# Eight weight images and the first routed tokens: a list scheduler's order for the work ahead of the first expert block

## The chip, the core and the metric

The kernel runs on one core of a Trainium2 chip. The metric is device time in microseconds (us) of one execution. Five engines work side by side, each through its own instruction stream: TensorE (PE; its weight loads are listed as PEld), VectorE (DVE), ScalarE (ACT), GpSimd (POOL) and SyncE (SP). Here SP mostly issues DMAs. An instruction waits at the head of its engine's stream until what it needs is there, and everything behind it in that stream waits too.

## What is computed

```python
# x: 8 x 3584 x 192, 8 heads of 24 columns, 7 taps per head
w = softmax(weight)                         # per head, over the 7 taps
out = np.einsum('hk,bskhg->bshg', w, x_unf) # causal convolution along the sequence
x = out.reshape(28672, 192)
logits = normalised(x) @ normalised(expert_emb).T / tau
expert_idx = np.argmax(logits, axis=1)      # one of 8 experts per token
gate_w = softmax(logits)[expert_idx]
for e in range(8):
    h = np.maximum(x[mask] @ w1[e], 0.0)    # 192 -> 1024
    out[mask] = gate_w[mask, None] * (h @ w2[e])  # 1024 -> 192
```

All inputs are fp32. The kernel multiplies in 16-bit floats: tokens, weights and hidden values are each scaled by a power of two and split into a high and a low half, and the products that matter are summed.

## The kernel before, in words

**Tokens.** The 28,672 tokens are 16 chunks of 1,792 (`CT`), each 16 tiles of 112. `mix` convolves a chunk: one matmul per head (L416) with a banded 128 x 112 matrix (`band`), copied back by ACT (L421); then the squares of each row (ACT L428, DVE L431) and an inverse root by a chain of small DVE instructions (L137 to L148, L440 to L444). `route` scales the chunk (DVE L460), casts the high half (ACT L462), subtracts for the low half (DVE L464, L467), turns the rows round (TensorE transposes L491 and ACT copies L495 for chunks 0 and 1, DMA transposes L617 for the others), multiplies with the expert vectors (L499), ranks (L518 to L573, ending in `di`, the target row of every token), and queues 16 scatters: GpSimd's indirect DMAs (L621) write each token's halves into `rows_d` in DRAM, sorted by expert.

**Experts.** `select` picks blocks of 128, 256, 512 or 1,024 rows of one expert, as soon as enough are there (`hand_out` after the chunk counts in `PICK`, the first after two chunks; `last_blocks` at the end). It leaves a table `sel` with the offset of the expert's weights and of the rows. `fetch` reads the row offset into a register of SP and issues a DMA transpose into `e_xT` (L741), which waits for the scatters it needs. `expert` runs one block: `flip` copies half of `e_xT` (L763), `copy_w1` and `copy_w2` copy the expert's images from `res` into the single `slot` (L723, L726) at an address in a DVE register that `value_load` (L720) has read from `sel`. Then h_ps (L796: five matmuls for 128 hidden columns), relu to a high half on ACT (L800) and the low half on DVE (L802), o_ps (L820: 24 matmuls for 128 rows), scaling by the gate (ACT L825) and a scatter into the output (POOL L827). The next block's W1 copy stands behind the last L802 of a block, its W2 copy behind the first steps of the next one.

**Weights.** For each expert SP loads W1 in two pieces and W2 (L290 to L292) into one of three staging buffers (parts of `slot`, `hid` and the end of `res`), so the load of expert e waits until expert e-3's images are finished. The sum of squares comes from matmuls (L321) and the diagonal (DVE L326; for the last four experts' W2 ACT squares), the scale from L156 to L162 and L334; the high half is written by ACT (L340), the low half by DVE (L344), both into `res`.

**What sets the order.** In `run` a hand-written interleaving (`HEAD`, `PRE`, `BEHIND`, `AHEAD`) issues weights, chunks 0 to 3 and a part of chunk 4 in turn; the framework's own scheduler then orders each engine's stream, except SP's, which keeps the order of the code. Once the first blocks are picked, `expert` yields after each step how much DVE and ACT time is left under the matmuls; `dispatch` spends it on later chunks at a pace `rate`, and `tick` issues one scatter per `pace` steps, at least `SPACE` us apart by the code's own clock.

## Time and profile before

| | us |
|---|---|
| three runs | 1281.48, 1278.87, 1280.43; median 1280.43 |
| the profiled execution | 1279.59 |
| its span, first to last instruction | 1277.9 |
| TensorE busy | 1162.7 (91%) |
| VectorE busy | 865.4 (68%) |
| ScalarE busy | 584.3 (46%) |
| GpSimd busy | 554.9 (43%) |

The span is what the profile's rows divide; 1.7 us of the execution lie around it. A matmul's listed time overlaps that of the next, so the distance of two starts is what a matmul costs in a row of them. "Idle before" is the time an engine stood still ahead of an instruction, with what ended it behind the arrow. `x_p_s` is a chunk's scale, `w_p_s` a weight's, `n` or `n2` a sum of squares.

### The profile page before, as it was taken

The numbers are of one execution on the slowest core, as the hardware profiler recorded it, in microseconds if no ns is written. First come the engines' busy times: TensorE is split into PE (matmuls) and PEld (weight loads), VectorE is DVE, ScalarE is ACT, GpSimd is POOL, SyncE is SP. The second block draws the span as 40 slices with busy tenths as digits, with TensorE's granted clock in tenths as the row PEclk, the third lists the DMA queues.
The fourth block names the chain that finished last, engine by engine and source line by source line (L and its number), as shares of the span: only waits on it lengthen the run. The fifth ranks groups of instructions, "written<-read, shape, count | busy, mean of one in ns | idle before, by whom it ended". The sixth has DMA issues, their size and how long they took to land. (4 is left out here: it accounts for less than half of the span.)

```text
span 1277.9 us, 29782 instructions
## 1 busy us (share of the span) xinstructions
PE 1162.7 (91%) x10852; PEld 927.9 (73%) x10852; DVE 865.4 (68%) x2274; ACT 584.3 (46%) x1343; POOL 554.9 (43%) x541
## 2 busy tenths in 40 slices
PE   4664689999999989999999989999999999999997
PEld 2542578788888878768886757667777777779997
DVE  2967758687877786857777566766644465466675
ACT  3967343544635444553545544543333333333332
POOL 0055054455555555455455544555555221223222
PEclk9666699999999999999999989999999999999999
DMA  9564536446454644645464256534323121111211
GB/s 261 149 195 115 109 91 118 105 107 150 98 124 103 138 100 111 157 101 124 93 137 114 87 125 139 110 90 92 80 65 82 43 52 38 45 38 42 49 43 23
DMA packets 274290, 129.15 MB, mean 101 GB/s; under 512 B 216110, under 2 KB 264621, under 8 KB 274144
## 3 DMA queue, kind: packets, MB, share of 16 engines
q1 hardware_dynamic: 250336, 80.39, 29.4%
q0 software_dynamic: 23808, 46.87, 12.9%
q8 instruction: 85, 1.39, 0.5%
q14 instruction: 61, 0.50, 0.2%
HBM read 38.35 MB, written 47.53 MB: 67 GB/s over the span
## 5 line engine op out<-in xcount | busy, mean ns | idle before, releaser
L820 PE MATMUL o_ps<-slot,hid 128*128 128x192 f16 x5544 | 500.9, 248 | 32.5 <-DVE hid L802 11.0
L820 PEld LDWEIGHTS <-hid 128*128 128x128 f16 x5544 | 460.6, 99 | 75.1 <-DVE hid L802 22.6
L796 PE MATMUL h_ps<-e_xT,slot 128*128 128x256 f16 (+2 forms) x3168 | 499.4, 292 | 10.9 <-DMA e_xT<-rows_d 7.3
L796 PEld LDWEIGHTS <-slot 128*128 128x128 f16 x3960 | 351.6, 99 | 168.8 <-issue 22.7
L827 POOL DMA_INDIRECT out_dram<-y,e_mt x231 | 267.0, 1156 | 432.8 <-ACT y L825 384.7
L802 DVE SCALAR_TENSOR_TENSOR hid<-h_ps,hid 128x512 f16<-128x512 f32 x462 | 310.1, 687 | 142.1 <-ACT hid L800 107.2
L800 ACT ACTIVATE hid<-h_ps 128x512 f16<-128x512 f32 x462 | 269.0, 597 | 220.0 <-PE h_ps L796 189.3
L621 POOL DMA_INDIRECT rows_d<-rows,di x256 | 269.6, 1053 | 226.0 <-PE h_ps L796 58.5
L796 PE MATMUL h_ps<-e_xf,slot 128*128 128x256 f16 (+2 forms) x792 | 219.0, 291 | 0.4 <-issue 0.4
L825 ACT ACTIVATE y<-o_ps,g 128x192 f32<-128x192 f32 x231 | 94.5, 420 | 266.7 <-PE o_ps L820 225.9
L726 DVE COPY slot<-res 128x3074 f16 x99 | 96.9, 979 | 120.3 <-PE o_ps L820 94.3
L416 PE MATMUL conv_ps<-xt,band 128*112 128x384 f32 x256 | 112.5, 548 | 18.7 <-ACT xt L421 7.4
L421 ACT COPY xt<-conv_ps 112x384 f32<-112x384 f32 x128 | 59.8, 479 | 84.4 <-PE conv_ps L416 49.1
L723 DVE COPY slot<-res 128x3072 f16 x99 | 94.2, 952 | 0.0
L462 ACT CAST rows<-xt 112x768 f16<-112x768 f32 x64 | 53.2, 832 | 85.7 <-DMA rows_d<-rows,di 60.7
L464 DVE TENSOR_TENSOR rows<-xt,rows 112x512 f16<-112x512 f32 x64 | 44.2, 691 | 45.8 <-ACT rows L462 41.0
L499 PEld LDWEIGHTS <-xT 128*112 128x112 f16 x768 | 55.8, 146 | 24.8 <-DMA xT<-rows 15.5
L416 PEld LDWEIGHTS conv_ps<-xt,band 128*112 128x112 f32 x256 | 43.3, 198 | 39.2 <-issue 16.8
L499 PE MATMUL lg_ps<-ma,xT 128*112 128x16 f16 x512 | 55.5, 202 | 15.8 <-DMA xT<-rows 14.1
L428 ACT ACTIVATE sq<-xt 112x192 f32<-112x192 f32 x192 | 68.3, 359 | 2.8 <-DVE sq L431 1.4
L460 DVE TENSOR_TENSOR xt<-xt,x_p_s 112x768 f32<-112x768 f32 x64 | 58.3, 951 | 0.2 <-issue 0.2
L763 DVE COPY e_xf<-e_xT 64x256 f16<-64x256 f16 (+2 forms) x198 | 46.5, 235 | 13.4 <-DMA e_xT<-rows_d 9.1
(163 smaller groups left out, 539.4 us busy)
## 6 DMA issues: line engine op xcount, KB each, us to landing
xt<-in_dram SPq DMA_DIRECT2D x39, 384.0 KB
xt<-in_dram SPq DMA_DIRECT2D x3, 1440.0 KB
rows_d<-rows,di POOLq DMA_INDIRECT x256
res<-in_dram SPq DMA_DIRECT2D x5, 768.0 KB
out_dram<-y,e_mt POOLq DMA_INDIRECT x231
xT<-rows SPq DMA_TRANSPOSE x224
xt<-in_dram SPq DMA_DIRECT2D x2, 1536.0 KB
hid<-in_dram SPq DMA_DIRECT2D x3, 768.0 KB
```

Source lines behind the costliest of these rows:

```text
L416: i = nc.tensor.matmul(out=ps, lhsT=self.band[:, h, :], rhs=xt[:, :, h * G:(h + 1) * G], start=True, stop=True).ins
L428: nc.scalar.activation(out=sq, in_=xc[:, t, :], func=AF.Square, accum_out=n2[:, t:t + 1])
L499: i = nc.tensor.matmul(out=lg[:, g * GX + a, :], lhsT=xT[:, a, k, :], rhs=self.mb if k == 1 else self.ma, start=(k == 0), stop=(k == 2)).ins
L621: i = self.nc.gpsimd.indirect_dma_start(out=self.rows_d[:, :], out_offset=bass.IndirectOffsetOnAxis(ap=idx, axis=0), in_=src, in_offset=No ...
L723: self.under(nc.vector.tensor_copy(out=self.slot[:, 0:W2], in_=v).ins)
L726: self.nc.vector.tensor_copy(out=self.slot[:, W2:], in_=self.res[:, bass.ds(self.we + W2, RES - W2)])
L796: self.mm = nc.tensor.matmul(out=ps[:, c, :], lhsT=w1(o, b + c), rhs=xk[k], start=(i == 0), stop=(i == 4)).ins
L800: self.step = nc.scalar.activation(out=hh[:, b:b + m, :], in_=ps, func=AF.Relu).ins
L802: self.low = nc.vector.scalar_tensor_tensor(out=hl[:, b:b + m, :], in0=ps, scalar=0.0, in1=hh[:, b:b + m, :], op0=ALU.max, op1=ALU.subtrac ...
L820: self.mm = nc.tensor.matmul(out=o, lhsT=h[:, c, q], rhs=w2[:, c, k:k + D], start=(c + i == 0), stop=(c == NFC - 1 and i == 2)).ins
L825: self.step = nc.scalar.activation(out=y, in_=o, func=AF.Copy, scale=g[:, a:a + 1]).ins
L827: i = nc.gpsimd.indirect_dma_start(out=self.out[:, :], out_offset=bass.IndirectOffsetOnAxis(ap=mt[:, a, 0:1], axis=0), in_=y, in_offset=No ...
```

## The change

The work ahead of the first block is now described as nodes: `chunk` and `weights` add each piece with its engine, a duration, what it needs and a priority, and `_Plan.run` repeatedly takes the node that could start first by these numbers and issues it. TensorE, VectorE and ScalarE keep that order. This head holds chunks 0 and 1 with their 32 scatters, of chunk 2 only the convolution, squares and root, all eight weights, the first pick and the first W1 copy; chunk 3 and a part of chunk 4 are no longer in it.

`res` becomes two tensors, `res1` for W1 and `res2` for W2. Expert e's weights are loaded into the place that expert e+2's images will take (the last two into `slot` and `hid`), so that no load waits for a staging buffer; the loads of x for chunks 2 and 3 wait for the splits of chunks 0 and 1. W1's last 64 rows come as 128 x 512. Chunks 0 and 1 in the head are cast with the scale on ACT, one tile per instruction, and DVE subtracts from the scaled product with two instructions per tile; nothing is scaled beforehand. Chunk 2 is turned round by TensorE as well. The first pick is followed by up to three 128-row blocks (`MORE`). The register load for a block is one instruction less and is tied behind the last L802 of the block before it, next to its copy.

```diff
-PRE = 14, 8
-BEHIND = 4
-HEAD = 9, 8, 9, 4, 2, 2, 2, 2
-AHEAD = 0.4
...
-MARGIN = 22
+MARGIN = 30
 KMAX = 32
+MORE = 3
+EAGER = 4
+DIRECT = 2
+FLIP = 1.5
+GRAMS = 4
...
+RANKS = 0.0, 0.28, 5.0
+ORDER = 0, ~0, ~1, 1, 2, ~2, 3, 4, 5, 6, ~3, 7
+PITCH = 1.4
+LATE = 1.0
+PICKED = 0.0
+ACTS = 6, 2, 14
 LAND_X, LAND_T = 9.0, 4.5
...
-SPACE, EVICT, SAVED = 1.65, 0.6, 8.0
+SPACE, EVICT, SAVED = 1.54, 0.6, 8.0
+SIGNAL, MOVED = 0.15, 1.8
+DONE = 2.6, 7.9
...
+    def run(self):
+        left = self.nodes
+        while left:
+            at = [(t + n.pri, k, t) for k, n in enumerate(left)
+                  for t in (self.start(n),) if t is not None]
+            _, k, t = min(at)
+            n = left.pop(k)
+            for r in n.takes:
+                self.rings[r][1].append(n)
+            if n.emit:
+                n.emit()
+            n.end = self.free[n.engine] = t + n.us
...
-        self.res = self.cp.tile([128, E * RES], F16, name="res")
+        self.res1 = self.cp.tile([128, E * IMG], F16, name="res1")
+        self.res2 = self.cp.tile([128, E * IMG], F16, name="res2")
...
+        nc.scalar.dma_start(out=sd, in_=seq)
+        self.band, self.cseq = cp.tile([128, H, TP], F32, name="band"), sd
+
+    def load_band(self):
+        run = self.cseq[:, 0:TP]
+        self.nc.sync.dma_start(out=self.band, in_=bass.AP(
             tensor=run.tensor, offset=run.offset,
             ap=[[1, 128], [2 * 128, H], [1, TP]]))
...
+    def stage(self, e):
+        n = 3 * F
+        if e < E - 2:
+            o = (e + 2) * IMG
+            t = self.res1[:, o:o + n], self.res2[:, o:o + n]
+        else:
+            t = (self.slot, self.hid)[e - E + 2]
+            t = t[:, 0:n], t[:, n:2 * n]
+        return [v.bitcast(F32) for v in t]
...
+                nc.sync.dma_start(out=v["st"][:, 0:F], in_=self.w1[e][0:128, :])
+                w = self.w1[e][128:192, :]
+                nc.sync.dma_start(out=v["st"][:, F:F + F // 2], in_=bass.AP(
+                    tensor=w.tensor, offset=w.offset,
+                    ap=[[F // 2, 2], [F, 64], [1, F // 2]]))
...
+        l1 = P.add("SP", 0.8, lambda: load(0), after, pri=pri)
+        m1 = self.move(3.0, l1, pri)
+        l2 = P.add("SP", 0.4, lambda: load(1), l1, pri=pri)
+        m2 = self.move(3.0, l2, pri)
+        a = P.add("PE", 1.3, lambda: gram(0), m1, takes=("h",), pri=pri)
+        a = P.add("DVE", 0.38, lambda: diag(0), a, back=((a, "h"),), pri=pri)
+        if e < GRAMS:
+            b = P.add("PE", 1.2, lambda: gram(1), m2, takes=("h",), pri=pri)
+            b = P.add("DVE", 0.38, lambda: diag(1), b, back=((b, "h"),), pri=pri)
+        else:
+            b = P.add("ACT", 1.66, square, m2, pri=pri)
+        n = P.add("PE", 0.4, total, a, b, takes=("h",), pri=pri)
+        n = P.add("DVE", 0.6, scale, n, takes=("wp",), back=((n, "h"),), pri=pri)
+        s, lows = n, []
+        for k, (t, u) in enumerate(((1.1, 1.25), (0.7, 0.75), (0.7, 0.75),
+                                    (1.5, 1.8))):
+            late = pri + (LATE if k == 3 else 0.0)
+            h = P.add("ACT", t, lambda k=k: high(k), n,
+                      *(clear[3:] if k == 3 else clear[:3]), pri=late)
+            lows.append(P.add("DVE", u, lambda k=k: low(k), h, pri=late,
+                              back=((s, "wp"),)))
+        return lows, l2
...
+        def cast(g):
+            for t in range(g, g + GX):
+                self.mark = nc.scalar.activation(
+                    out=rows[:, t, 0:D], in_=xc()[:, t, :], func=AF.Copy,
+                    scale=v["s"][:, t:t + 1]).ins
+
+        def rest(g):
+            for t in range(g, g + GX):
+                for a, b, o in ((0, 128, 256), (128, 192, 192)):
+                    nc.vector.scalar_tensor_tensor(
+                        out=rows[:, t, o:o + b - a], in0=xc()[:, t, a:b],
+                        scalar=v["s"][:, t:t + 1], in1=rows[:, t, a:b],
+                        op0=ALU.mult, op1=ALU.subtract)
...
+        subs, lgs, first = [], [], None
+        for g in range(0, NT, GX):
+            n = P.add("ACT", 1.3, lambda g=g: cast(g), s, pri=pri)
+            subs.append(P.add("DVE", 1.35, lambda g=g: rest(g), n, pri=pri))
...
+        for t in range(NT):
+            n = P.add("POOL", PITCH, lambda t=t: send(t), n, pri=pri)
+            sent.append(n)
+        return subs, done, sent
...
-    def route(self, c, xbar):
+    def route(self, c):
...
-            if xbar and 0 < g <= 2 * GX:
+            if c > DIRECT and 0 < g <= 2 * GX:
...
-        self.we = nc.vector.value_load(sel[0:1, j, 0:1], min_val=0,
-                                       max_val=(E - 1) * RES)
-        v = self.res[:, bass.ds(self.we, W2)]
+        (i,), (self.we,) = nc.values_load_multi_w_load_instructions(
+            sel[0:1, j, 0:1], engines=[nc.vector.engine], min_val=0,
+            max_val=(E - 1) * IMG, skip_runtime_bounds_check_because="select clamps it")
+        self.under(i.ins)
+        v = self.res1[:, bass.ds(self.we, W2)]
         self.under(nc.vector.tensor_copy(out=self.slot[:, 0:W2], in_=v).ins)
 
...
-            out=self.slot[:, W2:], in_=self.res[:, bass.ds(self.we + W2, RES - W2)])
+            out=self.slot[:, W2:], in_=self.res2[:, bass.ds(self.we, IMG)])
...
             0, -((E * (n - 1) - self.left) // n))
+        k = min(k, most)
...
+    def head(self, first):
+        P = self.plan = _Plan(
+            dict(h=5, r=2, l=1, x=2, root=1, wp=2),
+            dict(PE=8.6, DVE=8.8, ACT=7.6, SP=2.0, DMA=2.3, POOL=3.3))
+        moved, subs, ranked, sent = [], [], [], []
+        self.line, low = (), []
+        at = P.add("SP", 0.0, None)
+        self.banded = P.add("DMA", 0.0, None, lag=MOVED)
+        for k, v in enumerate(ORDER):
+            if k == 1:
+                at = P.add("SP", 0.4, self.load_band, at)
+                self.banded.after = self.move(2.5, at, 0.0),
+            if v >= 0:
+                l, at = self.weights(v, at, low[v - 2] if v > 1 else (), TURNS[v])
+                low.append(l)
+                continue
+            c = ~v
+            at = P.add("SP", 0.9, lambda c=c: self.load_x(c), at,
+                       *(subs[c - 2] if c > 1 else ()), pri=1.0)
+            moved = [self.move(5.4, at, 1.0)]
+            if c < first:
+                u, r, t = self.chunk(c, moved, RANKS[c], ACTS[c], ranked)
+                subs.append(u)
+                ranked.append(r)
+                sent += t
+            elif c == first:
+                self.chunk(c, moved, RANKS[c], ACTS[c], ranked)
+
+        def pick():
+            self.left = first * CT
+            self.hand_out(first)
+
+        def more():
+            self.subs += sum(self.pick(128, most=MORE), [])
+
+        n = p = P.add("DVE", 3.8, pick, ranked[-1], pri=PICKED)
+        for _ in range(3):
+            n = P.add("SP", 2.0, lambda: self.fetch(), n, *sent, at)
+        n = P.add("DVE", 1.3, lambda: self.copy_w1(0), p,
+                  *[v for l in low for v in l[:3]])
+        P.add("DVE", 4.2, more, n, *[l[3] for l in low], pri=2.0)
+        P.run()
+        self.asked = {c: -LAND_X for c in range(4)}
+        self.sp_at = 0.0
+
...
-        self.now = self.counts[c]
+        self.now, self.need = self.counts[c], NT * c
...
-        self.rate = min(self.rate, 3.0)
+        self.rate = 3.0 if self.end <= EAGER else min(self.rate, 3.0)
...
+        with self.tc.manual_schedule(engines={
+                e.tensor.engine, e.vector.engine, e.scalar.engine}):
+            self.head(first)
+        a, spent = self.dispatch(first), list(DONE)
```

`_Node` holds a piece's engine, duration, emitter, predecessors, buffer rings and priority; the emitters that the cut leaves out issue the instructions named above. Over the whole program TensorE's matmul transposes go from 96 to 144 and DMA transposes of x from 224 to 208; W1 and W2 copies go from 99 to 101 each (128-row blocks 21 to 25, 256-row blocks 51 to 49, 512-row pieces 27 as before); the output tiles stay 231 and the scatters of tokens 256.

SyncE at the start, before (`xt` is a chunk of x, `cseq_d` and `band` make the banded matrix, the others are weights):

```order
L369 DMA xt<-in_dram 112x192
L378 DMA xt<-in_dram 128x15x192
L227 DMA cseq_d<-cseq 8x256
L290 DMA slot<-in_dram 128x1024
L291 DMA slot<-in_dram 64x1024
L292 DMA res<-in_dram 128x8x192
L231 DMA band<-cseq_d 128x8x112
L290 DMA hid<-in_dram 128x1024
L291 DMA hid<-in_dram 64x1024
L292 DMA hid<-in_dram 128x8x192
L378 DMA xt<-in_dram 128x16x192
```

and after (`res_94` is `res1`, `res_95` is `res2`):

```order
L381 DMA res_94<-in_dram 128x1024
L383 DMA res_94<-in_dram 128x1x512
L377 DMA res_95<-in_dram 128x8x192
L310 DMA band<-cseq_d 128x8x112
L470 DMA xt<-in_dram 112x192
L479 DMA xt<-in_dram 128x15x192
L479 DMA xt<-in_dram 128x16x192
L381 DMA res_94<-in_dram 128x1024
L383 DMA res_94<-in_dram 128x1x512
L377 DMA res_95<-in_dram 128x8x192
L381 DMA res_94<-in_dram 128x1024
```

The band now follows the first weight, and x of chunks 0 and 1 come behind it, ahead of the second weight; the write of `cseq_d` has gone to ScalarE's queue.

VectorE at the first block, before:

```order
L344 SCALAR_TENSOR_TENSOR res<-hid,w_p_s,res 128x8x192
L723 ISA
L723 COPY slot<-res 128x3072
L148 SCALAR_TENSOR_TENSOR x_r_y<-x_r_t,x_r_y 112x16
L518 TENSOR_REDUCE l<-lg_ps 112x128
L726 ISA
L726 COPY slot<-res 128x3074
L763 COPY e_xf<-e_xT 64x256 x2
```

and after:

```order
L434 SCALAR_TENSOR_TENSOR res_94<-hid,w_p_s,res_94 64x512 x2
L434 SCALAR_TENSOR_TENSOR res_94<-slot,w_p_s,res_94 64x512 x2
L1094 COPY e_xf<-e_xT 64x256 x2
L1049 TENSOR_LOAD sel_3584_1058
L1054 ISA
L1054 COPY slot<-res_94 128x3072
L434 SCALAR_TENSOR_TENSOR res_95<-hid,w_p_s,res_95 128x8x192
L434 SCALAR_TENSOR_TENSOR res_95<-slot,w_p_s,res_95 128x8x192
L985 TENSOR_TENSOR sl_av<-cb_1025,start 1x8
L1133 SCALAR_TENSOR_TENSOR hid<-h_ps,hid 128x512
```

The flip of the fetched rows (`e_xf`) now stands ahead of the first W1 copy, and two low halves of W2 stand behind that copy, ahead of the first L802 (L1133 after the change).

VectorE at a 128-row block near the end, before:

```order
L811 TENSOR_SCALAR g<-e_mt,slot 128x1
L802 SCALAR_TENSOR_TENSOR hid<-h_ps,hid 128x512 x2
L723 ISA
L723 COPY slot<-res 128x3072
L763 COPY e_xf<-e_xT 64x128 x2
L726 ISA
```

and after:

```order
L1142 TENSOR_SCALAR g<-e_mt,slot 128x1
L1133 SCALAR_TENSOR_TENSOR hid<-h_ps,hid 128x512 x2
L1049 TENSOR_LOAD sel_1920_14585
L1054 ISA
L1054 COPY slot<-res_94 128x3072
L1094 COPY e_xf<-e_xT 64x128 x2
```

A TENSOR_LOAD now stands between the block's last low half and the W1 copy; before, the registers had been read in bunches behind each `select`.

## Rows read from the trace of the kernel before

**Rows 1.** Windows of all engines: length, busy us (x instructions), granted clock, DMA share, GB/s.

```profile
0.00:147.50 147.50, 81.64 (x510) 55.84 (x511) 99.66 (x332) 94.04 (x207) 39.61 (x57) 0.69 0.61 173
147.50:250.00 102.50, 94.15 (x899) 81.10 (x899) 69.42 (x208) 43.06 (x106) 42.83 (x40) 0.96 0.47 99
250.00:1000.00 750.00, 721.77 (x6527) 566.43 (x6527) 529.36 (x1440) 349.40 (x844) 395.82 (x379) 0.99 0.48 109
1000.00:1278.00 278.00, 265.10 (x2919) 224.50 (x2916) 166.99 (x294) 97.77 (x187) 76.68 (x65) 1.00 0.18 41
```

**Rows 2.** Timeline (start us, us, engine, line, operation, idle before), TensorE, first expert matmuls.

```profile
147.56 3.15 PE L796 MATMUL h_ps<-e_xT,slot 128*128 128x256 f16 x14 [2.64 <-DMA e_xT<-rows_d]
```

**Rows 3.** Waits in 0 to 147.5 us, SyncE queue: total us, times, longest.

```profile
SPq L290 <- DVE res L344: 42.7, 4, 18.2
```

**Rows 4.** Timeline, TensorE, first convolution.

```profile
16.69 7.00 PE L416 MATMUL conv_ps<-xt,band 128*112 128x384 f32 x16 [2.64 <-issue]
```

**Rows 5.** Groups by form, VectorE, 0 to 147.5 us: count, busy us, mean ns, idle before.

```profile
L460 DVE TENSOR_TENSOR xt<-xt,x_p_s 112x768 f32<-112x768 f32 x16 | 14.5, 949 | 0.2 <-issue 0.2
L464 DVE TENSOR_TENSOR rows<-xt,rows 112x512 f16<-112x512 f32 x16 | 11.0, 689 | 0.0
L467 DVE TENSOR_TENSOR rows<-xt,rows 112x256 f16<-112x256 f32 x16 | 6.8, 423 | 0.0
L344 DVE SCALAR_TENSOR_TENSOR res<-hid,w_p_s,res 128x1024 f16<-128x1024 f32 x3 | 3.9, 1285 | 0.0
L344 DVE SCALAR_TENSOR_TENSOR res<-res,w_p_s 128x1536 f16<-128x1536 f32 x5 | 9.0, 1802 | 0.1
L326 DVE SCALAR_TENSOR_TENSOR w_dg<-tr_ps,idf 128x128 f32<-128x128 f32 x12 | 3.5, 289 | 24.9 <-ACT sq L428 10.3 <-remote 8.9 <-PE tr_ps L321 5.2
```

**Rows 6.** Timeline, GpSimd, two scatters of chunk 1, the later one its last.

```profile
106.17 0.94 POOL L621 DMA_INDIRECT rows_d<-rows,di  x1 [0.31 <-issue]
...
117.35 1.42 POOL L621 DMA_INDIRECT rows_d<-rows,di  x1 [0.30 <-issue]
```

**Rows 7.** Timeline, SyncE queue, first fetch of a block.

```profile
144.41 1.24 SPq L741 DMA_TRANSPOSE e_xT<-rows_d  x1
```

**Rows 8.** Timeline, VectorE, the longest idle stretch after 30 us.

```profile
91.76 0.29 DVE L326 SCALAR_TENSOR_TENSOR w_dg<-tr_ps,idf 128x128 f32<-128x128 f32 x1 [7.90 <-remote]
```

**Rows 9.** Timeline, TensorE: one head of a convolution, twelve logit matmuls, eight transposes.

```profile
59.07 0.91 PE L491 MATMUL tr_ps<-idh,rows 112*128 112x112 f16 x8
...
194.67 0.17 PE L499 MATMUL lg_ps<-ma,xT 128*112 128x16 f16 x1
...
195.22 0.20 PE L499 MATMUL lg_ps<-ma,xT 128*112 128x16 f16 x1
...
730.58 0.82 PE L416 MATMUL conv_ps<-xt,band 128*112 128x384 f32 x2
731.24 1.98 PE L820 MATMUL o_ps<-slot,hid 128*128 128x192 f16 x22
```

**Rows 10.** Timeline, VectorE, around register loads.

```profile
816.34 0.18 DVE L145 TENSOR_TENSOR x_r_t<-x_r_y 112x16 f32<-112x16 f32 x1 [0.52 <-DVE x_r_y L148]
...
822.53 0.69 DVE L802 SCALAR_TENSOR_TENSOR hid<-h_ps,hid 128x512 f16<-128x512 f32 x1 [0.36 <-issue]
823.41 0.69 DVE L802 SCALAR_TENSOR_TENSOR hid<-h_ps,hid 128x512 f16<-128x512 f32 x1 [0.19 <-issue]
```

**Rows 11.** Timeline, VectorE, W1 copies behind a 256-row and a 128-row block.

```profile
1172.19 0.95 DVE L723 COPY slot<-res 128x3072 f16 x1
...
1191.40 0.95 DVE L723 COPY slot<-res 128x3072 f16 x1
```

**Rows 12.** Timeline, TensorE, first matmuls of the blocks behind those copies.

```profile
1174.71 0.39 PE L796 MATMUL h_ps<-e_xT,slot 128*128 128x128 f16 x4
...
1192.40 0.29 PE L796 MATMUL h_ps<-e_xT,slot 128*128 128x128 f16 x2
```

**Rows 13.** Waits in 147.5 to 1278 us, TensorE for fetched rows.

```profile
PE h_ps L796 <- DMA e_xT<-rows_d: 7.3, 3, 4.2
```

479 lines of the change are left out of this document (327 added, 152 removed).

## The prediction

> **What bounds the kernel now.** I read the windows first, then TensorE's timeline at their seams, then the waits, the groups by form and single timelines. The windows [rows 1] part the span in two. Up to 147.5 us no engine is full: TensorE 82 us busy, VectorE 100, ScalarE 94, at a granted clock of 0.69 on average. Then the first expert block starts [rows 2], and TensorE sets the pace: 1081.0 of 1130.5 us busy. Its 49.5 us of idle time are 8.4 to 250 us, 28.2 over the 750 us in which later chunks are worked in, and 12.9 after 1000 us. So a microsecond taken off the head is a microsecond off the span, unless it only moves TensorE's work behind 147.56, where it comes back one to one.
>
> Why the head is long: SP's queue holds weight loads back until a staging buffer is free, 42.7 us in four waits [rows 3], and VectorE, with the most work, is idle for 147.5 - 99.7 = 48 us.
>
> **The head, worked out.** Two chains end at the first block, and I count both.
>
> VectorE. Of its 99.7 us of work [rows 1] half of four chunks' scaling and subtracting leaves the head: (14.5 + 11.0 + 6.8)/2 = 16.2 [rows 5], and with chunk 3's squares and root some 4 more. The two chunks that stay change form: before 8.1 us a chunk; now 32 instructions of 112 x 128 and 112 x 64. The nearest row is the 128 x 128 form at 0.29 [rows 5]; two at that price are 9.3 us a chunk, at 0.29 and half of it 7.0. I take 8, no change. The weights' low halves cost what they cost: 1.29 for W1's first part, as much for its two halves of 64 rows, 1.80 for W2, 4.4 an expert. That leaves 79.5 us. W0's low halves (4.4) now run while x is on its way; the rest, 75 us, needs chunk 0's convolution. That began at 16.69 and took 7.00 [rows 4]; the band is now issued behind one weight and ahead of x, where before two weights and x surrounded it, so I leave the start at 16.7 (15 to 18). 23.7 + 75 = 98.7. The start-up's small instructions, which I have left in the 75, stand for the idle time that remains. Before, there were 48 us of it; the loads that caused most of it wait no more.
>
> Scatters. The last nine of chunk 1 took (117.35 - 106.17)/8 = 1.40 each [rows 6], 32 take 45 us. Ahead of chunk 0's `di` stand in VectorE's new order its own split (8) and squares, root and rank (about 9), of chunk 1 the squares and a quarter of its split, and one W1: some 25 us, with a few of waiting `di` at 51. 51 + 45 = 96. The fetch took 147.56 - 144.41 = 3.15 [rows 7, 2]. Then, by the new order, the flip of the fetched rows, the register load and the first W1 copy (0.95, [rows 11]) follow on VectorE in turn, 1.7 together, where before the copy was long done. 96 + 3.2 + 1.7 = 101.
>
> Both chains say about 100; I take 101 for the first h_ps, 94 to 112. Gain: 147.56 - 101 = **46.5 us**.
>
> **What comes back behind it.**
> - TensorE work that had been in the head: chunk 2's 48 logit matmuls: twelve start within 0.55 us (194.67 to 195.22, [rows 9]), 0.6 with the last, so 2.4; its rows are turned by 48 TensorE transposes instead of DMAs, 0.70/8 = 0.088 each in the head [rows 9], where the mean clock was 0.69 of full [rows 1], so 2.1 (if it was the lower of the levels, 1.2 against 2.4 GHz) to 4.2, I take 3.0; chunk 3's eight heads at 0.66 (730.58 to 731.24, [rows 9]), 5.3; three heads of chunk 4, 2.0. Sum **+12.7**.
> - The two W2 low halves behind the first W1 copy delay the first block's low halves by 2 x 1.80. Five PSUM banks cover part: **+2** (0 to 4).
> - Working in chunks costs TensorE idle time: (8.4 + 28.2)/13 = 2.8 for each of the 13 chunks worked in by then. About 1.75 chunks' work more: +4.9. Against it, `MARGIN` 22 to 30 lets scatters end earlier, and of 7.3 us of waits for fetched rows the longest is 4.2 [rows 13]: -4. The bunches of register loads behind each `select` are gone from VectorE; of some 100 loads at a quarter microsecond I give back a tenth, -3 (0 to -8). Sum **-2**.
> - Each load now stands between a block's last low half and the next W1 copy. A load shows as 0.52 us between two dependent instructions, and as 0.19 behind a long one [rows 10]. A 256-row block has room: its copy ends at 1172.19 + 0.95 = 1173.14 and the next block starts at 1174.71 [rows 11, 12]. A 128-row block has none: copy from 1191.40, h_ps at 1192.40, as soon as it ends. So it is paid at the 25 blocks of 128 rows: 25 x 0.19 = 4.8 to 25 x 0.52 = 13. Behind the long low half the shorter price is the nearer one; at 0.25, **+6**.
> - Two blocks more (four more of 128, two fewer of 256), each exposing a W1 copy of 0.95: **+2**.
>
> At nothing I cost the split of `res` in two (the copies keep their size), the SP issues (SP is not waited for once the loads flow) and ScalarE's finer casts: 94 us busy in the head before, less two chunks' casts and copies, it has room below VectorE's end.
>
> Sum: -46.5 + 12.7 + 2 - 2 + 6 + 2 = **-25.8**. The profiled execution took 1279.6 (span 1277.9 and 1.7 around it), 0.8 less than the median of the runs shown: 1279.6 - 25.8 = 1253.8, so **1254**.
>
> The Trainium skill has a figure that speaks against this change: "DMA: Bandwidth & Descriptors", section "Latency and other measured facts", gives a register load a floor of about 600 ns. By it the 25 loads would cost 15 and the sum would be 1263. The rows here are below it, 0.52 at most, so the trace does not agree and decides.
>
> **Rivals.**
> - *The queue at block ends is dearer.* Each load stops VectorE in full, 25 x 0.52 = 13 instead of 6; the new work in the first blocks (chunk 2's split, ranks and scatters, chunk 3's convolution) crowds VectorE and ScalarE, and TensorE's idle time to 200 us doubles from about 8. -25.8 + 7 + 8 = -10.8: 1269. For it: VectorE is 68% busy from 147.5 to 250 even before. Against: it has more room where blocks of 256 follow one another.
> - *The head does better.* First h_ps at 94, loads hidden but for 0.1 each, idle time per chunk falls by half a microsecond: -25.8 - 7 - 3.5 - 6 = -42: 1237. For it: if VectorE never waits, its chain ends at 92 to 94. Against: the scatters' 1.40 is a floor from the same trace and ends at 96 unless `di` comes sooner than 51.
> - *Slower: stalls under dense loads.* One idle stretch of 7.90 us hit VectorE with a releaser that the profile cannot name [rows 8]. Now all loads run densely from the start. If such stalls come with loads in flight, four of them (31.6) exceed the 25.8: 1285. Four is the point from which it decides; one in 147 us, none other as long in the head, speaks against four in a head of 100.
> - *It doesn't arrive.* The first hand-out is 7 blocks of 256 and 3 of 128 rows, 17 output tiles; 231 tiles in 1130.5 us are 4.9 each, so it lasts 83 us at most. Chunk 2 must have its 16 scatters out by then; before, it was ranked soon after the first block. If chunk 2's rows came 25 us late, TensorE would stand that long: 1279. Against: its scatters take 16 x 1.54 = 25 by `SPACE`, so there are over 50 us for the rest.
>
> **How the numbers follow.** About 0.2% (2.6 us) is what a measurement of this kernel can tell from no change. Forecast 0.55 (own range 1244 to 1264), dearer block ends 0.20, better head 0.14, stalls 0.06, gain not arriving 0.05. Faster: the first three and a little of the last, 0.90; same 0.04; slower 0.06. The unknown ends (first h_ps 94 to 112, loads 4.8 to 13, idle time) span from 1237 to 1272; leaving a tenth on each side gives 1238 to 1270.
>
> **What would show it.** First h_ps near 101 and chunk 0's convolution still from about 16.7; no wait of SP's loads for low halves but for x of chunks 2 and 3; the last scatter of chunk 1 near 96, and flip, load and W1 copy in turn behind the fetch; no second stall like the 7.90 one; near the end 0.2 to 0.3 between a 128-row block's last low half and its W1 copy, and the next h_ps later by as much; TensorE's idle time from the first block on near 50 to 60. If the first h_ps comes after 115, or that idle time passes 75, the sum is wrong, and the step is named by which of the two it is.

## The result, and the profile after

The change was forecast at 1254 us (1238 to 1270) and came out slower than before: 1290.8 us (median of 14 runs, 1279.5 to 1295.1) against 1281.0 for the kernel before, measured with it (14 runs), a ratio of 1.0056 (95% interval 1.0036 to 1.0075). The profiled execution took 1287.05, its span 1285.3.

The windows of the kernel after the change, cut at its first expert matmul, with the columns of [rows 1]:

```profile
0.00:132.00 132.00, 58.89 (x410) 43.08 (x410) 88.46 (x340) 76.94 (x147) 42.86 (x55) 0.71 0.57 172
132.00:250.00 118.00, 101.96 (x956) 83.60 (x957) 95.73 (x313) 66.20 (x191) 43.44 (x42) 0.89 0.41 97
250.00:1000.00 750.00, 724.96 (x6567) 568.28 (x6565) 527.82 (x1425) 349.20 (x831) 392.70 (x379) 0.99 0.49 109
1000.00:1285.30 285.30, 272.86 (x3021) 231.69 (x3018) 172.76 (x305) 99.95 (x191) 78.52 (x66) 1.00 0.19 42
```

The first window should end near 101 and ends at 132: the head became 15.4 us shorter [rows 2], not 46.5. TensorE is 22.7 us less busy in it than before [rows 1], and what was moved is paid behind it: from the first block to the end it is 1285.3 - 132.2 = 1153.1 us, against 1130.3 before. That is 22.8 more, where 20.7 were forecast (+12.7 +2 -2 +6 +2). Nearly the whole surprise, 31 us of 33, is in the head. VectorE has 88.5 us of work there and stands still for 43.5, nearly as long as before (48), though no weight load waits for a staging buffer any more [rows 3].

What keeps it waiting is seen in the windows of 10 us (the same columns):

```profile
70.00:80.00 10.00, 6.79 (x62) 6.16 (x61) 8.66 (x25) 8.60 (x15) 6.98 (x6) 0.50 0.68 202
80.00:90.00 10.00, 3.14 (x16) 1.70 (x16) 2.74 (x10) 3.66 (x4) 3.55 (x4) 0.50 0.85 259
...
100.00:110.00 10.00, 0.61 (x4) 0.34 (x4) 2.11 (x3) 4.78 (x6) 1.69 (x2) 0.50 0.09 28
```

From 80 to 90 and again from 100 to 110 us the five engines do little: VectorE is busy 2.7 and 2.1 us of 10. The timeline of the kernel after the change around these two holes, lines of all engines in order of time (start, us, engine, line, operation, idle before; SPq is SyncE's DMA queue):

```profile
80.85 1.03 PE L392 MATMUL tr_ps<-slot 128*128 128x128 bf16 x8 [2.30 <-DMA slot<-in_dram]
...
83.49 6.35 SPq L381 DMA_DIRECT2D hid<-in_dram  x1
...
87.57 0.61 PE L392 MATMUL tr_ps<-slot 128*128 128x128 bf16 x4 [5.68 <-DMA slot<-in_dram]
87.98 0.21 PE L681 MATMUL pc_ps<-rc,lth 112*128 112x8 f16 x1
...
88.28 0.17 DVE L687 TENSOR_TENSOR off<-pc_ps,cb 112x8 f32<-112x8 f32 x1 [7.12 <-PE pc_ps L681]
...
89.89 0.53 SPq L383 DMA_DIRECT2D hid<-in_dram  x1
...
102.66 0.61 PE L392 MATMUL tr_ps<-hid 128*128 128x128 bf16 x4 [5.37 <-DMA hid<-in_dram]
...
105.17 1.48 ACT L401 ACTIVATE hid<-hid 128x1536 f16<-128x1536 f32 x1 [13.15 <-DMA hid<-in_dram]
...
106.65 4.09 ACT L429 ACTIVATE res<-res,w_p_s 128x1024 f16<-128x1024 f32 x4
...
107.82 2.84 DVE L434 SCALAR_TENSOR_TENSOR res<-res,w_p_s 128x1024 f16<-128x1024 f32 x3 [8.19 <-ACT res L429]
...
108.68 1.24 POOL L950 DMA_INDIRECT rows_d<-rows,di  x1 [8.23 <-ACT res L429]
...
124.43 1.22 POOL L950 DMA_INDIRECT rows_d<-rows,di  x1 [0.30 <-issue]
...
127.31 1.34 SPq L1072 DMA_TRANSPOSE e_xT<-rows_d  x1
...
130.42 0.46 DVE L1094 COPY e_xf<-e_xT 64x256 f16<-64x256 f16 x2 [5.59 <-DMA e_xT<-rows_d]
131.15 0.96 DVE L1054 COPY slot<-res 128x3072 f16 x1 [0.28 <-DVE e_xf L1094]
132.17 1.03 PE L1127 MATMUL h_ps<-e_xT,slot 128*128 128x256 f16 x4 [4.71 <-DVE slot L1054]
```

In both holes TensorE waits for the second piece of a W1, the one that L383 loads: eight of the twelve matmuls of its sum of squares have run, the last four stand 5.68 and 5.37 us longer. Everything queued behind them stands too. At 87.57 these are chunk 1's rank sums (`pc_ps`), and with them VectorE (7.12 us). At 102.66 the queue is ScalarE's: the square of the last weight's W2, loaded behind that W1, has held ScalarE for 13.15 us, so the high halves behind it come late, for these VectorE waits 8.19 us and GpSimd, whose scatters are tied to ScalarE's order, 8.23. The last scatter starts at 124.43, and from the fetch on it goes as forecast: fetch, flip, copy, matmul, 4.86 us from 127.31 to 132.17 (3.15 + 1.7 forecast, [rows 7, 11]).

Why the second piece comes late is seen in windows of 1 us near the start, when the rest of the first weight has landed and only this piece is under way. After the change:

```profile
7.00:8.00 1.00, 0.58 (x6) 0.32 (x3) 0.00 (x0) 0.00 (x0) 0.00 (x0) 1.00 0.98 257
...
9.00:10.00 1.00, 0.00 (x0) 0.00 (x0) 0.00 (x0) 0.00 (x0) 0.00 (x0) 1.00 0.13 50
```

The last two columns: a DMA share of 0.13, what two fully busy ones of the 16 DMA engines make (2/16 = 0.125), at 50 GB/s. At that rate a piece of 256 KB takes 5.2 us (an estimate: 262,144 bytes at 50 GB/s), eight times in the head. The diff had it in plain sight: the source of L383 is `[[F // 2, 2], [F, 64], [1, F // 2]]`, two halves of a row outermost. The Trainium skill states the rule ("DMA: Bandwidth & Descriptors", section "Why a DMA increments its semaphore by 16 and not by 1"): the number of engines is the largest, up to 16, that divides the size of the slowest dimension (longer than one) of both sides. That makes two here, whatever the 128 partitions of the destination would allow. The trace agrees with its 0.13. The forecast had not put this load to that rule.

### The profile page after: what moved, and what is told of

Read it like the earlier page. It is cut to its first block, busy times and chain, and to the rows that moved or that the text cites. A ratio compares the mean times of both kernels' runs of the same rounds, so it can differ in the third digit from the quotient of the medians.

```text
span 1285.3 us, 29875 instructions
## 1 busy us (share of the span) xinstructions
PE 1158.7 (90%) x10948; PEld 926.7 (72%) x10948; DVE 884.8 (69%) x2381; ACT 592.3 (46%) x1359; POOL 557.5 (43%) x541
## 4 chain that ended last, share of the span: by engine, by line
PE 31%; issue 28%; POOL 10%; DVE 10%; ACT 4%; DMA 3%; SPq 2%; another core or an unknown queue 1%; POOLq 1%; DVEq 0%; ACTq 0%
PE h_ps L1127 15%; PE o_ps L1151 12%; POOL out_dram L1158 8%; PE conv_ps L751 3%; POOL rows_d L950 3%; DVE xt L795 2%; DMA rows_d<-rows,di 2%; DVE hid L1133 2%; ACT sq L763 1%; SPq L946 1%; PE lg_ps L832 1%; DVE rows L799 1%; ACT hid L1131 1%; DMA xT<-rows 1%
## 5 line engine op out<-in xcount | busy, mean ns | idle before, releaser
L1127 PE MATMUL h_ps<-e_xT,slot 128*128 128x256 f16 (+2 forms) x3232 | 506.9, 291 | 12.2 <-DVE slot L1054 5.6
L1133 DVE SCALAR_TENSOR_TENSOR hid<-h_ps,hid 128x512 f16<-128x512 f32 x462 | 310.7, 687 | 133.2 <-ACT hid L1131 106.7
L751 PE MATMUL conv_ps<-xt,band 128*112 128x384 f32 x208 | 85.3, 503 | 0.0
L797 ACT CAST rows<-xt 112x768 f16<-112x768 f32 x56 | 46.3, 833 | 83.8 <-DMA rows_d<-rows,di 50.2
L799 DVE TENSOR_TENSOR rows<-xt,rows 112x512 f16<-112x512 f32 x56 | 38.7, 691 | 47.8 <-ACT rows L797 38.2
L756 ACT COPY xt<-conv_ps 112x384 f32<-112x384 f32 x104 | 49.1, 479 | 46.3 <-PE conv_ps L751 33.6
L763 ACT ACTIVATE sq<-xt 112x192 f32<-112x192 f32 x156 | 55.3, 358 | 1.6 <-DVE sq L766 0.4
L832 PEld LDWEIGHTS <-xT 128*112 128x112 f16 x672 | 45.2, 134 | 10.0 <-issue 3.7
L795 DVE TENSOR_TENSOR xt<-xt,x_p_s 112x768 f32<-112x768 f32 x56 | 51.0, 950 | 0.0
L832 PE MATMUL lg_ps<-ma,xT 128*112 128x16 f16 x448 | 44.2, 194 | 3.2 <-issue 2.0
L832 PE MATMUL lg_ps<-mb,xT 128*112 128x16 f16 x224 | 38.1, 197 | 1.0 <-issue 0.8
```

What stands on the lines that cost most here:

```text
L751: i = nc.tensor.matmul(out=ps, lhsT=self.band[:, h, :], rhs=xt[:, :, h * G:(h + 1) * G], start=True, stop=True).ins
L795: nc.vector.tensor_tensor(out=xc[:, u, :], in0=xc[:, u, :], in1=sb, op=ALU.mult)
L832: i = nc.tensor.matmul(out=lg[:, g * GX + a, :], lhsT=xT[:, a, k, :], rhs=self.mb if k == 1 else self.ma, start=(k == 0), stop=(k == 2)).ins
L1127: self.mm = nc.tensor.matmul(out=ps[:, c, :], lhsT=w1(o, b + c), rhs=xk[k], start=(i == 0), stop=(i == 4)).ins
L1133: self.low = nc.vector.scalar_tensor_tensor(out=hl[:, b:b + m, :], in0=ps, scalar=0.0, in1=hh[:, b:b + m, :], op0=ALU.max, op1=ALU.subtrac ...
```

## The experiments

The kernel before takes 1250 to 1253 us on two of the chips used and 1281 to 1286 on the others, so times are compared as ratios to it on the same chip, with 95% intervals; a difference of two rows from different batches is less certain than one within a batch. "First h_ps" is the start of the first expert matmul in the profiled execution, in us.

| run | what it is | us | ratio to before, same chip | first h_ps |
|---|---|---|---|---|
| two_loads | change, W1's last rows by two DMAs | 1249.9 | 0.999 [0.9952, 1.0029] | 114.5 |
| no_marks | change, scatters free of ScalarE | 1260.3 | 1.0065 [1.0034, 1.0096] | 128.8 |
| both | these two | 1250.5 | 0.9995 [0.9964, 1.0025] | 120.0 |
| before_two | before, with such a source for W1 | 1269.4 | 1.0154 [1.0078, 1.0229] | 155.6 |
| after_again | the change, second chip | 1268.7 | 1.0137 [1.0092, 1.0181] | 133.1 |
| before_again | before, second chip, one run | 1255.1 | | 139.5 |
| x_first | two loads, x ahead of the first weight | 1253.3 | 1.0005 [0.9983, 1.0027] | 120.8 |
| no_more | two loads, no small extra blocks | 1253.2 | 1.0003 [0.9983, 1.0023] | 114.9 |
| pairs | change, source's 64 rows outermost | 1272.4 | 0.9904 [0.9872, 0.9935] | 116.4 |
| pin | two loads, flip behind the copy | 1267.6 | 0.9843 [0.9811, 0.9876] | 115.8 |
| x_pin | pin and x first | 1270.8 | 0.9884 [0.9858, 0.991] | 116.7 |
| x_pin_nomarks | these and free scatters | 1277.6 | 0.9931 [0.9905, 0.9956] | 122.0 |
| two_loads_b | two_loads, fourth batch | 1271.4 | 0.9904 [0.9876, 0.9931] | 117.8 |
| bunched | two loads, register loads as before | 1279.2 | 0.9968 [0.995, 0.9986] | 116.3 |
| pin_b | pin, fourth batch | 1266.8 | 0.987 [0.9843, 0.9896] | 115.9 |
| x_pin_b | x_pin, fourth batch | 1268.9 | 0.9898 [0.9867, 0.9929] | 117.8 |

Each group of four rows from the top (the first to the fourth batch) ran on one chip.

**Is it the shape of the load?** `two_loads` moves nothing but this: the same bytes to the same places in two DMAs of 64 partitions.

```diff
-                w = self.w1[e][128:192, :]
-                nc.sync.dma_start(out=v["st"][:, F:F + F // 2], in_=bass.AP(
-                    tensor=w.tensor, offset=w.offset,
-                    ap=[[F // 2, 2], [F, 64], [1, F // 2]]))
+                for i in range(2):
+                    nc.sync.dma_start(out=v["st"][64 * i:64 * i + 64, F:F + F // 2],
+                                      in_=self.w1[e][128:192,
+                                                     i * F // 2:(i + 1) * F // 2])
```

> The changed kernel, with W1's last 64 rows loaded by two DMAs of 64 x 512 each instead of one of 128 x 512 whose source has two outer rows; nothing else moves on any engine. Theory 1 (few engines): the single DMA is spread over two of the 16 DMA engines only, since its 2048-byte packets start at some 22 a microsecond (45 GB/s) while the 4096-byte packets of the other W1 piece start at 70 to 100 (290 GB/s and more); it takes 6 us for each of eight weights, and W7's last piece lands near 104 us for that. Then the pieces land within about 1 us, the last weight near 75 to 80, the first h_ps falls from 132 to between 100 and 110, and the time by 20 to 30 us. Theory 2 (order of the streams): the loads are only dense, and the head is late because scatters and rank sums stand behind instructions that wait for weights; then this changes less than 5 us.

In the changed head each scatter but a chunk's first is tied behind the last ScalarE instruction issued before it (`mark`). The rival at this point was that these ties, and not the load, made the holes. `no_marks` takes the ties alone away; `both` has this edit and the two loads:

```diff
-                _dep(self.tc, self.scatters[-1], self.mark.name)
+                pass
```

> The changed kernel without the dependency of each head scatter on the last ScalarE instruction issued before it; the loads as in the change. Theory 2: scatters no longer wait for ScalarE's high halves (8.2 us at 108 in the profile of the change), chunk 1's last scatter comes at 110 to 114 instead of 124 and the first h_ps at 120 to 125, the time falls by 6 to 10 us. Theory 1: the weights' low halves themselves end near 125 because W7 lands at 104, so the W1 copy can't come before 125 and the gain is at most 6 us.

> Two loads and no dependency of the scatters on ScalarE. Theory 1: little beyond the two loads alone (0 to 4 us), since ScalarE then waits for nothing long: 22 to 32 us below the change. Theory 2: 6 to 12 us below the change, like the scatters alone.

And the suspected shape, put into the kernel before:

```diff
-        nc.sync.dma_start(out=s1[0:64, F:2 * F], in_=w1[128:192, :])
+        w = w1[128:192, :]; nc.sync.dma_start(out=s1[0:64, F:2 * F], in_=bass.AP(tensor=w.tensor, offset=w.offset, ap=[[F, 2], [2 * F, 32], [1, F]]))
```

> The kernel before, with the 64-row piece of W1 read through a source of two outer rows (2 x 32 rows, interleaved, so the rows land in another order and the weights are permuted: the output is not the reference's). Same bytes, same DMA count, same order on every engine. Theory 1: these eight DMAs of 256 KB run on two engines, 6 us each instead of under 1; the head gets longer by 5 to 20 us (the loads come in threes behind the staging ring, where part of it is hidden), and the time with it. Theory 2: under 2 us.

With two loads the first h_ps comes at 114.48, later than the 100 to 110 expected. The windows of `two_loads` from 70 to 110 us:

```profile
70.00:80.00 10.00, 6.42 (x58) 5.58 (x55) 9.50 (x30) 9.52 (x13) 7.43 (x8) 0.67 1.01 318
80.00:90.00 10.00, 2.29 (x16) 2.05 (x16) 9.30 (x33) 5.19 (x9) 7.87 (x8) 0.50 0.26 78
...
100.00:110.00 10.00, 6.33 (x16) 2.73 (x14) 6.84 (x11) 9.90 (x16) 6.74 (x5) 0.88 0.15 47
```

The holes are gone (VectorE 9.30 where it had 2.74), the DMAs move 318 GB/s from 70 to 80 instead of 202, and the last weight is issued at 64.20, where it was 83.49. The kernel before, given such a source, loses 1.5% (four runs), and its first h_ps comes at 155.6 where `before_again` has 139.5. The ties alone are not the cause: without them and with the slow load the kernel stays slower than before (1.0065). They make the slow load worse, though: 1.0065 is some 9 us less than the 1.0137 that `after_again` shows on a like chip, where at most 6 were expected if the load is the cause. With the load mended they cost nothing that shows (0.9995 against 0.999).

The first h_ps alone doesn't give the time. In `both` it comes 5.5 us later than in `two_loads`, and the time is level: behind it TensorE is busy for 1085.4 us instead of 1091.9. Its granted clock from there to 250 us is 0.95 in `both` and 0.93 in `two_loads`.

**On one chip, with the head's remaining parts.** `after_again` and `before_again` are the two kernels unchanged.

> The changed kernel, unchanged, on the chip of the next two. Theory 1 (W1's 64 rows on two DMA engines): 8 to 18 us slower than the same kernel with two loads, so some 0.6 to 0.8% slower than before, with the first h_ps 14 to 18 us later than with two loads. Theory 3: on a chip without the stalls it is still slower than before by as much, since the loads and not the stalls make the head long.

> The kernel before, unchanged, profiled beside the others. The first profile of before shows idle time with no releaser (issue, remote) of 13.5 us on TensorE and 66 on VectorE; the runs with two loads, 2.4% faster in all on their chip, show next to none. Theory 3 (the stalls belong to the chip): if this run's time is near 1250, these waits are gone here too, the first h_ps comes at 136 to 142 instead of 147.6, and some 1112 us lie behind it; if it is near 1280, they are there again. Theory 4 (they belong to the kernel's instructions): they are there in either case.

`x_first` has the two loads and brings x of chunk 0 ahead of the first weight:

```diff
-ORDER = 0, ~0, ~1, 1, 2, ~2, 3, 4, 5, 6, ~3, 7
+ORDER = ~0, 0, ~1, 1, 2, ~2, 3, 4, 5, 6, ~3, 7
...
-            if k == 1:
+            if k == 2:
```

> Two loads, and x of chunk 0 as SP's first load, W0 behind it, then the band. With two loads chunk 0's convolution starts at 19.0 after waiting 7.0 us for x; before the change it started at 16.7. Theory 5 (the first convolution sets the scatter chain, which sets the first h_ps): the convolution starts at 14 to 17, the first scatter 2 to 5 us before 58.4, the first h_ps 2 to 5 us before 114.5, the time 2 to 5 us below two loads. Rival: VectorE's weights set it, W0 comes later, and the gain is under 1 us.

`no_more` has the two loads and gives the small blocks up again:

```diff
-MORE = 3
+MORE = 0
```

> Two loads without the up to three 128-row blocks behind the first hand-out. Theory 6 (each extra block costs an exposed W1 copy): 2 to 3 us faster than two loads. Rival: the blocks fill a hole in which the rows of chunk 2 are not yet there; without them TensorE waits for fetched rows, and the time is 3 to 10 us longer.

Here the change is slower than before by 1.4%, while the mended one in the batch before was level: 1.4 to 1.5%, some 18 us, come from one source shape, and the first h_ps tells the same (133.1 and 114.5, 18.7 apart). That is twice the 0.6 to 0.8% expected. `before_again` has its first h_ps at 139.5, 8 us earlier than in the rows shown before: the stretch of 7.90 us [rows 8] isn't there on this chip. `x_first` does start the scatters 3.2 us earlier than `two_loads` (55.29) and the last of them 2.1 earlier (104.61), but its first block comes 6.3 us later; the time is level, not the 2 to 5 us shorter that were expected. Its VectorE timeline shows what stands ahead of the first W1 copy:

```profile
103.40 0.15 DVE L234 TENSOR_SCALAR w_p_e<-n_ps 128x2 int32<-128x2 int32 x1
110.26 0.46 DVE L1094 COPY e_xf<-e_xT 64x256 f16<-64x256 f16 x2 [6.70 <-DMA e_xT<-rows_d]
...
111.10 1.82 DVE L434 SCALAR_TENSOR_TENSOR res<-hid,w_p_s,res 128x1536 f16<-128x1536 f32 x1
112.84 2.84 DVE L434 SCALAR_TENSOR_TENSOR res<-slot,w_p_s,res 128x1024 f16<-128x1024 f32 x3
115.71 0.96 DVE L1054 COPY slot<-res 128x3072 f16 x1
```

The flip of the fetched rows stands in VectorE's stream in the middle of the last weights' scale and low halves. VectorE waits 6.70 us for the fetch and then still has 5 us of weight work ahead of the first W1 copy. The extra small blocks cost nothing that shows (1.0003 without them, 0.999 with them on another chip, each within 0.2 to 0.4%). But that is a balance of two things, since the rival's hole is there. TensorE's waits in `no_more`:

```profile
PE h_ps L1127 <- DMA e_xT<-rows_d: 12.2, 2, 11.7
```

Without the blocks TensorE stands 11.7 us for fetched rows; in `two_loads` it never waits for them. Behind the first h_ps it is idle for 50.7 us in `no_more` and 43.4 in `two_loads`, and busy for 1085.3 and 1091.9: the blocks bring about as much work as they fill.

**The outer dimension or the 128 partitions, and the flip.** `pairs` keeps one DMA to 128 partitions and only swaps the source's outer dimensions:

```diff
-                    ap=[[F // 2, 2], [F, 64], [1, F // 2]]))
+                    ap=[[F, 64], [F // 2, 2], [1, F // 2]]))
```

> The changed kernel with one source of W1's last 64 rows turned: the outer dimension is the 64 rows and the two halves of a row lie inside, so a row's halves land on neighbouring partitions (the images of W1's last rows are then wrong: the output is not the reference's). One DMA, 128 x 512, the same bytes, the same order on every engine. Theory 1, sharpened (the number of DMA engines follows from the outer dimension of the source, 2, and not from the 128 partitions it fills): as fast as two loads, 0.999 of before within 0.4%, first h_ps near 115. Rival (a load onto 128 partitions with 2-KB packets is slow by its form): like the change, 1.014 of before.

`pin` has the two loads and ties the first flip behind the weights' low halves and the first W1 copy:

```diff
-            nc.vector.scalar_tensor_tensor(
+            self.tail = nc.vector.scalar_tensor_tensor(
...
+        i = nc.vector.tensor_copy(out=self.slot[:, 0:W2], in_=v).ins; self.under(i); self.tail = self.tail if self.gated else i
...
-            self.under(nc.vector.tensor_copy(
-                out=xf[o:o + 64, :], in_=xT[i:i + 64, 1, :]).ins)
+            i = nc.vector.tensor_copy(out=xf[o:o + 64, :], in_=xT[i:i + 64, 1, :]).ins
+            self.flips or _dep(self.tc, i, self.tail.name, False); self.under(i)
```

`tail` is the last low half, and then the first W1 copy; the wait is for the flip alone.

> Two loads, with the first flip of fetched rows held behind the weights' last low halves and the first W1 copy on VectorE. With two loads VectorE stood 5.6 us at that flip waiting for the fetch, with 0.3 + 0.96 of W1 copy and 3.6 us of W2 low halves behind it. Theory 7 (the flip in front of the copy holds up the first block): first h_ps 1.2 us earlier than 114.5, the first blocks' low halves 3 to 4 us earlier, the time 2 to 5 us below two loads. Rival: the scatters and the fetch set it alone, under 1.5 us.

`x_pin` is `pin` with the order of `x_first`, and `x_pin_nomarks` takes the ties away as well.

> x of chunk 0 first and the flip held behind. With x first alone the fetch was there at 110.3, but VectorE had waited 6.7 us at the flip with 9 us of W6's low halves and the copy behind it, and h_ps came at 120.8. Theory 7: h_ps at 110 to 112, the time 6 to 10 us below x first and 3 to 7 below two loads: 0.993 to 0.996 of before. Rival: ScalarE's high halves for W6, which came at 111 only, were late by themselves; then nothing is gained.

> As x first with the flip held behind, and the scatters free of ScalarE. The last scatter came at 104.6 with x first although 32 of them take 45 us from 55.3, so some 4 us are waits for ScalarE. Theory 2's remainder: last scatter at 100 to 102, h_ps at 106 to 109 if VectorE's weights allow it, 1 to 4 us below x_pin. Theory 1 alone: no change.

One DMA with 64 outermost is as good as two (first h_ps 116.4, ratio 0.9904, the same as `two_loads_b` on another such chip): it is the source's outer dimension, not the 128 partitions, the 2-KB packets or the number of DMAs. The 0.999 expected was a ratio of the other kind of chip. `pin` has the shortest median of its batch. x first gains nothing with it either (first h_ps 116.7, not 110 to 112): the W1 copy is done at 113.4 there, and TensorE comes to the first h_ps straight from convolutions of chunks 2 and 3 (112.31 to 116.73), so the flip no longer sets it. Free scatters make it worse, 0.9931 against 0.9884, where a gain was expected.

**What the other parts are worth.** Still open by then: whether the register loads cost (as forecast) or gain, and whether `pin` repeats beside the mended change on one chip. `bunched` is `two_loads` with the loads in bunches behind `select` again:

```diff
-        (i,), (self.we,) = nc.values_load_multi_w_load_instructions(
-            sel[0:1, j, 0:1], engines=[nc.vector.engine], min_val=0,
-            max_val=(E - 1) * IMG, skip_runtime_bounds_check_because="select clamps it")
-        self.under(i.ins)
+        self.we = nc.vector.value_load(sel[0:1, j, 0:1], min_val=0,
+                                       max_val=(E - 1) * IMG)
```

> The kernel with two loads again, as the base of the next three on one chip. 0.990 of before if the chip has the stalls without a releaser (before near 1280 to 1286), 0.999 if it has not (before near 1250).

> Two loads, with the register loads read as before the change: with the bounds check, and free for the scheduler, which puts them in bunches behind each select. The prediction's price (0.25 us at each of 25 small blocks, less 3 for the bunches): 3 us faster than two loads. What the trace of the change shows (the W1 copy starts in the last low half's shadow at 96 of 101 blocks, so the load costs nothing there): the same or 1 to 4 us slower than two loads, as the bunches are back.

> Two loads and the flip held behind, beside two loads on one chip. Theory 7: 2 to 5 us faster than two loads. Rival: under 1.5 us.

> x first and the flip held behind. Where the chip has the stalls, x_pin was 0.4% slower than pin, which its order of the head does not explain; if that was the stalls falling in its head, then on a chip without them it is the fastest of all, 5 to 9 us below two loads with the first h_ps at 109 to 112. If it is again behind pin there, the earlier start of chunk 0 is worth nothing because VectorE's weights end late.

`bunched` is 7.8 us slower than `two_loads_b`, more than any of the expectations: the loads beside their copies gain about 8 on this chip. TensorE's waits in the main part (from 118 us on: us, times, longest) for `bunched`:

```profile
PE o_ps L1151 <- DVE hid L1133: 21.3, 33, 2.7
PE o_ps L1151 <- ACT hid L1131: 14.2, 9, 4.8
```

and for `two_loads_b`:

```profile
PE o_ps L1151 <- DVE hid L1133: 16.6, 25, 2.6
PE o_ps L1151 <- ACT hid L1131: 5.8, 9, 1.5
```

The largest differences of the two traces are waits for hidden values from VectorE and ScalarE. `pin_b` is 4.5 us faster than `two_loads_b` (1265.1 to 1269.8 against 1267.7 to 1275.2). Its VectorE timeline at the first block:

```profile
108.39 1.53 DVE L434 SCALAR_TENSOR_TENSOR res<-slot,w_p_s,res 64x512 f16<-64x512 f32 x2
109.95 0.96 DVE L1054 COPY slot<-res 128x3072 f16 x1
110.83 1.81 DVE L434 SCALAR_TENSOR_TENSOR res<-hid,w_p_s,res 128x1536 f16<-128x1536 f32 x1
112.56 1.81 DVE L434 SCALAR_TENSOR_TENSOR res<-slot,w_p_s,res 128x1536 f16<-128x1536 f32 x1
...
115.82 0.46 DVE L1094 COPY e_xf<-e_xT 64x256 f16<-64x256 f16 x2 [1.39 <-DMA e_xT<-rows_d]
```

The W1 copy and both low halves of W2 now run while the fetch is under way. In `two_loads` VectorE stood 5.58 us for the fetch there, with this work behind it. `x_pin_b` repeats that x first adds nothing. The best version, `pin`, takes 0.984 to 0.987 of the time of the kernel before on the two chips where it ran, both of the slower kind; on one of the faster kind it was not run.

## Why the prediction was wrong, step by step

**The step that failed** is in the head's sum: "the SP issues (SP is not waited for once the loads flow)" cost nothing, and "the loads that caused most of it wait no more". The loads did stop waiting for buffers. But the step took every load to flow as before, and W1's last rows changed form; its new DMA was costed nowhere. It runs over two of 16 engines, and what SP issues behind it is issued later: the last weight at 83.5 instead of the 64.2 of `two_loads`. That is worth 18 to 19 us of head and about 1.5% of time. It is the largest of the head's misses and not the only one: with the load mended, the first h_ps is 25.1 us earlier than in `before_again` and the stretch behind it 21.4 us longer (1135.3 against 1113.9), so that hardly anything is left. "The weights' low halves cost what they cost" looked at VectorE's price of the new form alone: that was nearly right (1.51 for the two in the trace after, 1.29 forecast).

**The rest of the head's miss** is 114.5 - 101 = 13.5 us, seen in `two_loads`:

- Convolution of chunk 0: forecast from 16.7 to 23.7; its first matmul starts at 19.00 and its sixteenth ends near 26.8. The "15 to 18" for its start was too narrow: the band waits for `cseq_d` until 9.76, and x stands behind the band. 3 us, 2.3 of them from the later start.
- `di`: forecast at 51, the first scatter starts at 58.44. Of these 7.4 us the 3 are the convolution's and the others an estimate of VectorE's queue that was too short; it is full by then (9.3 to 9.6 of every 10 us from 30 to 70).
- VectorE's work: forecast at 79.5 us for the whole head, it is 88.6 up to the first h_ps, with two low halves of W2 (3.6) still behind it. Groups by form of `two_loads` up to 118 us show where it is more:

```profile
L612 DVE SCALAR_TENSOR_TENSOR rows<-xt,x_p_s,rows 112x128 f16<-112x128 f32 x32 | 11.0, 344 | 0.0
L612 DVE SCALAR_TENSOR_TENSOR rows<-xt,x_p_s,rows 112x64 f16<-112x64 f32 x32 | 8.9, 278 | 0.0
L538 DVE SCALAR_TENSOR_TENSOR drop<-xt 112x192 f16<-112x192 f32 x24 | 8.6, 357 | 9.6 <-ACT xt L527 8.9
```

  The split takes (11.0 + 8.9)/2 = 10 us a chunk, not 8: a form of half the width costs 278 ns beside 344, not half. And 24 squares of rows run on VectorE, with their sums 10.6 us, where 16 took 7.0 before: `ACTS = 6, 2, 14` in the diff moves them from ScalarE, and the forecast had only taken chunk 3's off.
- Scatters: 32 at 1.40 were 45 us; from 58.44 to the end of the last (106.71 + 1.25) it is 49.5, 1.55 each. 4.5 us more: 2.5 are one wait for ScalarE through the tie (2.83 us ahead of the eighth scatter, where 0.30 is usual), and without it the scatters take 1.47 each, a little more than the nine rows behind 1.40 [rows 6].
- Fetch behind the last scatter's end: 1.7 us that the sum left out. From the fetch on 4.84, as forecast.

The chain that bound was the scatters, which I had set equal with VectorE's. VectorE's ended close to it, also late: forecast at 98.7, in `two_loads` its work ahead of the flip was done at 107.1, and the flip waited. That the flip would stand ahead of the copy was in the forecast; that it holds 4.6 us of work behind a wait of 5.58 was priced at 1.7 and 2, and `pin` gets 4.5 back.

**Behind the head** the sum (+20.7) was right, its terms were not all: that it came out is partly luck. On the chip of the second batch, from the first h_ps on, it is 1113.9 us before and 1133.7 after, +19.8: TensorE's busy time +13.6 (forecast 12.7 of moved work), its idle time 39.3 to 45.5, +6.2 (forecast 8). The windows of `after_again` that this rests on:

```profile
133.10:250.00 116.90, 104.96 (x1052) 88.48 (x1053) 103.44 (x336) 68.59 (x197) 53.29 (x45) 0.94 0.46 107
250.00:1000.00 750.00, 727.37 (x6610) 571.49 (x6608) 528.89 (x1413) 353.36 (x838) 387.70 (x379) 1.00 0.49 108
1000.00:1266.80 266.80, 255.85 (x2882) 219.47 (x2879) 164.54 (x292) 93.32 (x179) 74.06 (x62) 1.00 0.19 43
```

and of `before_again`:

```profile
139.50:250.00 110.50, 106.50 (x1084) 95.20 (x1084) 86.04 (x250) 52.46 (x133) 54.16 (x50) 0.99 0.57 120
250.00:1000.00 750.00, 725.02 (x6551) 568.56 (x6549) 521.54 (x1413) 348.75 (x832) 388.65 (x377) 0.99 0.48 106
1000.00:1253.40 253.40, 243.04 (x2714) 207.20 (x2711) 157.84 (x281) 89.88 (x171) 69.61 (x58) 1.00 0.18 41
```

Idle time grew to 250 us, 4.0 to 11.9, and fell a little behind it, 25.0 to 22.6. So half of the rival of dearer block ends was right: the new work in the first blocks crowds VectorE (103.4 of 116.9 us busy, where it was 86.0 of 110.5), and TensorE waits there 8.2 us for its low halves, where it was 2.6. The clock goes with it: in TensorE's longest wait behind the first h_ps (3.16 us for ScalarE, until 208.78) the granted clock falls, to the lower level (0.50, 1.2 GHz) from 210 to 213 us, and over the window it is 0.94 against 0.99 before. That is up to 0.06 x 116.9 - 0.01 x 110.5 = 6 us (an estimate from these rows) of the 13.6 more of busy time, so the 12.7 forecast for moved work was met in part by something else. The rival's other half was not right:

- Register loads at block ends [rows 10]: priced +6, measured nothing. Of the 101 W1 copies 98 start without a gap behind the instruction ahead of them on VectorE, which at 81 of them is the last low half, as in this stretch of VectorE's timeline after the change, the load standing between the two:

```profile
1211.03 0.69 DVE L1133 SCALAR_TENSOR_TENSOR hid<-h_ps,hid 128x512 f16<-128x512 f32 x1 [0.42 <-ACT hid L1131]
1211.64 0.95 DVE L1054 COPY slot<-res 128x3072 f16 x1
```

  1211.03 + 0.69 is past the copy's start. The floor of about 600 ns that the Trainium skill states for a register load ("DMA: Bandwidth & Descriptors", section "Latency and other measured facts") isn't paid here. Whether a load takes that long beside the 0.69 us of the low half, no row shows.
- Bunches gone: priced -3, measured -8 (`bunched`, on a chip of the slower kind).
- Extra blocks: priced +2, none shows, as the balance above (`no_more`). Waits for fetched rows [rows 13]: none after.
- By these three the part behind the head should have come out 13 us below its forecast, and it didn't. Some of that may be the chip (`bunched` ran on one of the slower kind, the windows above are from one of the other); the 7.9 us of idle time in the first blocks are the part that I can show. What makes the rest is open.

**The other rivals.** The one on the slower side was stalls with no releaser; the time came out near its 1285, but not by it: no stretch like the 7.90 us one stands in the head after, and the holes there end with loads, each named. "Better head" had no part. "It doesn't arrive" had none with the extra blocks; without them its wait for fetched rows is there, 11.7 us (`no_more`), which the forecast didn't see: it counted "over 50 us for the rest". The signs I gave to watch did work: a first h_ps that "comes after 115" named the head, and a convolution later than 16.7 (20.80 in the trace after) was the first visible step of it.
